# Qk-normed attention with a maxout FFN on one Trainium2 core: seven running rows per partition, and a new order of moves in the first batch

## The chip, the core and the metric

The kernel runs on one core of one Trainium2 chip. The core has five engines that work side by side, each with its own instruction list, which it takes in order: TensorE (PE in the profile, with PEld for its weight loads) multiplies matrices, VectorE (DVE) and ScalarE (ACT) work on whole tiles, GpSimd (POOL) does elementwise work beside them, and SyncE (SP) issues transfers. A transfer (DMA) runs on 16 DMA engines. SBUF is the core's memory with 128 partitions; PSUM is the small memory into which TensorE writes. The metric is device time in microseconds, from several executions, of which the median counts.

## The reference

Eight batches, twelve heads, 448 tokens, 64 features per head. Queries and keys are RMS-normed, softmax attention gives x (3584 tokens by 768), and three layers with a maximum between them and one output layer follow.

```
q_n, k_n = (rmsnorm(q, g_q), rmsnorm(k, g_k))
scores = scale * np.matmul(q_n, k_n.transpose(0, 1, 3, 2))
scores = scores - np.max(scores, axis=-1, keepdims=True)
attn = np.exp(scores)
attn = attn / (np.sum(attn, axis=-1, keepdims=True) + 1e-09)
return np.matmul(attn, v).astype(np.float32)
...
h = np.maximum(np.maximum(x @ w1, x @ w2), x @ w3)
return (h @ w_out).astype(np.float32)
```

All inputs and the output are fp32.

## The kernel before

**Pairs and beats.** The twelve heads of a batch make six pairs (NP = 6), so there are 48 pairs g over eight batches. The main loop runs beat(g, i) for twelve beats i of each pair. A beat issues a little of everything: work on pair g, the rest of pair w = g - 1, the preparation of pair n = g + 2, loads for pair g + 3, and a slice of the FFN of the batch before (thirds, which takes steps from a queue of generators). `clock` counts beats, `later(b, work)` puts work b beats further on, and `tick` issues what is due. The order in which the calls are made is the order of each engine's list (a schedule written out by hand), so what is issued first also runs first on its engine.

**Precision.** Batch 0 (g < PLAIN = 6) runs attention in fp32: rows are turned by TensorE (turn_whole L527/L532, copied by keep_whole L543/L550), scores are L663, the maximum over them L693 (row_max), the exponentials L709 on ScalarE, their turning L729 (turn_plain) with copies L742/L745 (keep_turned), attention times values L840 (add_values). From batch 1 on each operand is split into an fp16 upper and lower part: upper_rows and lower_rows split queries and keys, turn_rows (L512) turns both parts of 128 partitions by one transposing transfer, swap_keys (L519) writes the keys a second time with the two parts exchanged, scores are L671 and L678, upper_weights (L796) and lower_weights (L806) split the weights of attention into pp, which has three buffers, turn_weights (L819 and, for the last block by halves of 64 partitions, L825) turns them into pt, and add_values is L851.

**Rows.** Two heads of 448 rows make 896 rows, seven blocks of 128. In load_rows (L386, L389) a partition p takes row p of each block, so its seven rows are 128 rows apart, 256 bytes each. load_v (L425, L430) loads values in blocks of 128 tokens, five transfers for three pairs' worth. Block 3 holds the last 64 rows of one head and the first 64 of the other.

**Norms.** For pair n: squares (L443 on GpSimd from pair 2 on, L441 on ScalarE before), sum_squares (L450 on VectorE), inv_rms (L460 and a power L464 on GpSimd), scale_rows (L472, L481 on GpSimd).

**Weights.** The 24 blocks of the weight matrices (18 of the first layer, six of w_out) are loaded raw and prepared one by one in prep_block: rebias (L182, ScalarE), three steps of decode on VectorE (L190, L194, L199), then a bound over the block from TensorE products with itself (marks: L274 for the first layer in bound_in, L253 for w_out in bound_block), a maximum (L162), its spread over the partitions (most: L283, L337) and from it the scale (w_up: a power L293 on GpSimd; by and o_up for w_out in bound_out, L333 to L352). With the scale a block is split into two fp16 parts: upper on ScalarE (L303, L358), lower on VectorE (L306, L363). BLOCK_BEATS gives the beats at which blocks begin: one each 4 beats for the first 18, then one each 8 beats, the first of them after beat 72.

**Bounds of the values.** largest_v (L586 on TensorE into marks, then L162) and bound_v (L591, spread L597, clear L602 and L606, scale L610 and L614) give each batch's scale for v.

**FFN.** layer1 (L880) accumulates 18 matmuls of 448 columns into a PSUM tile acc, of which there are three buffers shared with marks, most, rows, turned and spread. hidden takes three accumulators: the first is copied to m (L890, ScalarE), the second gives max(acc, m) in m (L894), the third gives the maximum in acc itself, from which ScalarE writes the upper half of the hidden tile ht (L900) and VectorE the lower (L904). GpSimd copies the last 64 columns of ht to hx (L909). layer2 (L942) multiplies by w_out, result (L951) scales to osb, store (L918) writes out. The FFN of batch 0 enters the queue at pair 6, beat 6, that is beat 78.

Of the kernel before, what the change touches and what calls it, by code (L numbers as in the profile page):

```python
# [17 lines left out]
P = 128  # L18
# [16 lines left out]

BLOCK_BEATS = (4, 8)

# [11 lines left out]
def qknorm_attention_maxout_ffn_kernel(  # L49
# [107 lines left out]

    sums = [const.tile([P, 2 * UNITS], F32, name=f"ss{i}") for i in range(2)]


# [67 lines left out]
    def prep_block(n):  # L228
        kind, ft, j = blocks[n]
        raw = raws[n]  # L230
        f = plain(w_sb, n) if kind == "in" else plain(wo_sb, ft)
        rebias(raw)

        for stage in range(3):
            later(2 + stage, lambda stage=stage: decode(raw, f, stage), True)
        if kind == "out":
            bound_block(ft, f)
        later(5 if kind == "in" else 9, load_raw)
        if j == NJ - 1:
            later(5, lambda: bound_in(ft), True)  # L240
        elif kind == "out" and ft == NFT - 1:
            later(8, bound_out, True)

    def bound_block(ft, f):

        box = []

        def products():
            box.append(ps_m.tile([P, 512], F32, name="marks", tag="m"))
            halves = f.bitcast(BF16).rearrange("p (n t) -> p n t", t=2)  # L250
            for c in range(NCT):
                part = halves[:, c * P:(c + 1) * P, 1]
                nc.tensor.matmul(  # L253
                    box[0][:, 0:P], part, part, start=c == 0, stop=c == NCT - 1
                )

        later(6, products)
        later(8, lambda: row_largest(o_row[:, ft:ft + 1], box[0][:, 0:P]), True)

    def bound_in(ft):  # L260
# [55 lines left out]

        for at, work in ((2, products), (4, reduce), (5, spread), (7, clear)):
            later(at, work)


    def bound_out():
# [50 lines left out]

        for at, work in ((2, across), (3, spread), (5, scale)):
            later(at, work)
# [28 lines left out]
    def load_v(t):  # L403
# [8 lines left out]
        if b == 0:  # L412
# [10 lines left out]
            return  # L423
        for u in range(3):
            nc.sync.dma_start(  # L425
                out=vr[:, :, u],
                in_=rows[:, u * P:(u + 1) * P].rearrange("h p d -> p h d"),
            )
        for half, part in zip(HALVES, (rows[:, 3 * P:S], rows[:, 0:LEFT])):
            nc.sync.dma_start(out=vr[half, :, 3], in_=part.rearrange("h p d -> p h d"))  # L430

# [71 lines left out]
    def turn_rows(g, what):  # L503
        s = st[g]
        parts = s.pop(what + "p")
        if what == "k":
            t = sb.tile([P, 2, UNITS * P], F16, name="kt", bufs=2)
            to = t[:, 0].rearrange("p (n r) -> p n r", n=UNITS)
        else:
# [79 lines left out]
    def bound_v(b):  # L589
# [25 lines left out]

        later(2, spread)
        if b < SQUARED:
            later(3, clear)
        later(5 if b < SQUARED else 3, scale)

# [34 lines left out]
    def scores(g, c):  # L655
# [4 lines left out]
        if g < PLAIN:  # L660
# [5 lines left out]
            return  # L666
        keys = (slice(0, S), slice(S, 2 * S))
        if c < 3:
            for h in range(2):
                for n in range(2):  # L670
                    nc.tensor.matmul(  # L671
                        sc[:, h, :S], qt[:, 4 * h + c], kt[:, n, keys[h]],
                        start=n == 0, stop=n == 1,
                    )
        else:
            for n in range(2):
                for h, rows in enumerate(HALVES):
                    nc.tensor.matmul(  # L678
                        sc[rows, 0, :S], qt[:, 3, rows], kt[:, n, keys[h]],
                        start=n == 0, stop=n == 1,  # L680
                    )
# [205 lines left out]
    def hidden(b, acc, hs, ft, j, keep):  # L887
# [28 lines left out]
    def store(b, osb, row0, token, n, cols=slice(0, DO), on=nc.sync):  # L916
        first = b * S + token
        on.dma_start(out=out[first:first + n, cols], in_=osb[row0:row0 + n, cols])  # L918

# [165 lines left out]
    def beat(g, i):  # L1085
        w, n = g - 1, g + 2
        c, part = divmod(i, 3)
        k = 4 * g + c
        early = k + 1 <= 4 * PLAIN
        if part == 0:  # L1090
            if g < G:
                if k > 4 * PLAIN:
                    row_max(g, c)
                softmax(g, c)
            if early:
                scores(*divmod(k + 1, 4))
            if 0 < k <= 4 * PLAIN:
                turn_plain(*divmod(k - 1, 4))
            elif 0 < k <= 4 * G:
                lower_weights(*divmod(k - 1, 4))  # L1100
        if part == 1:
            if 0 < k <= 4 * PLAIN:
                keep_turned(*divmod(k - 1, 4))
            if PLAIN <= g < G:
                upper_weights(g, c)
        if part == 2:
            if early:
                row_max(*divmod(k + 1, 4))
            elif k + 1 < 4 * G:
                scores(*divmod(k + 1, 4))  # L1110
        if 0 <= w < PLAIN:
# [14 lines left out]
        if w >= 0 and i == (9 if w < PLAIN else 10):  # L1126
            finish(w, x_of[w // NP])
# [19 lines left out]
        if PLAIN <= n < G and i == 11:  # L1147
            upper_rows(n, "k")
        if n < G:
            if i in (0, 3):  # L1150
# [8 lines left out]
        if g == 0 and i in (0, 3):  # L1159
            load_v(i // 3)  # L1160
            later(8, lambda: largest_v(i // 3))
# [3 lines left out]
        if g == 1 and i == 1:  # L1165
            bound_v(0)
        if g > 1 and g % NP == 0 and g < G and i == 1:
            bound_v(g // NP)
        if PLAIN <= g < G and i == 9:
# [15 lines left out]
        if PLAIN <= g < G and i in (5, 8, 11):  # L1185
            turn_weights(g, i // 3 - 1)
        n_in = min(decoded[0], NFT * NJ)
        due_at = BLOCK_BEATS[0] * n_in + BLOCK_BEATS[1] * (decoded[0] - n_in)
        if decoded[0] < len(blocks) and clock[0] > due_at:
            later(0, lambda n=decoded[0]: prep_block(n), True)  # L1190
# [43 lines left out]
```

## Time and profile before

| | |
|---|---|
| time, median of 3 runs | 1021.29 us (1019.76 to 1024.45) |
| the profiled execution | 1023.19 us |
| its span, first to last instruction | 1021.3 us |
| TensorE busy, VectorE busy | 983.2 us, 693.2 us |
| mean granted TensorE clock | 0.984 |
| packets of DMA | 519548, of them under 512 bytes 494436 |

The profile is of one execution. A group of instructions is given by line, engine, operation and tiles (out<-in), count, busy time and mean duration; behind the second bar stands the idle time of the engine just before, with what ended it. "Waits" name who waited for whom. The granted clock is the share of full speed that TensorE was given; matmuls are pipelined, so their durations overlap.

### The profile page before, as it was taken

The page shows a single profiled execution, that of the slowest core. Times are in us where ns is not written, and L with a number is a line of the kernel's source. Part 1 is how long each engine was busy: PE and PEld are TensorE (multiplying, and loading weights), DVE is VectorE, ACT ScalarE, POOL GpSimd, SP SyncE. Part 2 cuts the span into 40 slices and gives each one's busy share as a digit, 9 for nine tenths or more (in the row PEclk, how much of TensorE's full clock was granted, in tenths as well). Part 3 has the DMA queues.
Part 4 walks back from the last instruction along what each step waited for, and adds up shares of the span by engine and source line. Part 5 has one row for each costly group of instructions (what it writes and reads, how often), then busy time and mean ns, then how long its engine had stood idle before and what let it go on. Part 6 is the DMA issues. An engine that isn't in the chain of part 4 may idle for free. (4 is left out here: it accounts for less than half of the span.)

```text
span 1021.3 us, 17511 instructions
## 1 busy us (share of the span) xinstructions
PE 983.2 (96%) x6045; PEld 528.8 (52%) x6045; DVE 693.2 (68%) x1341; ACT 624.1 (61%) x1419; POOL 600.9 (59%) x659
## 2 busy tenths in 40 slices
PE   8987789899999999999999999999999999999998
PEld 5554444445555555555555555555555555555554
DVE  6998998788667767776677666776767757660120
ACT  6787776477566676666656675667666666651111
POOL 7666786567666576666676765776666657310000
PEclk9998799899999999999999999999999999999999
DMA  9955899979989899999989999999989998851001
GB/s 241 232 165 156 192 177 206 162 136 173 203 170 176 164 210 191 171 175 179 195 162 180 171 195 185 184 165 184 197 154 181 177 195 137 144 94 56 1 1 62
DMA packets 519548, 165.94 MB, mean 162 GB/s; under 512 B 494436, under 2 KB 515236, under 8 KB 519460
## 3 DMA queue, kind: packets, MB, share of 16 engines
q1 hardware_dynamic: 456480, 148.83, 75.3%
q10 hardware_dynamic: 62980, 16.00, 8.4%
q8 instruction: 48, 0.79, 0.3%
q14 instruction: 40, 0.33, 0.1%
HBM read 53.28 MB, written 11.01 MB: 63 GB/s over the span
## 5 line engine op out<-in xcount | busy, mean ns | idle before, releaser
L880 PE MATMUL acc<-xt,w_sb 128*128 128x448 f16 x2592 | 516.0, 354 | 3.6 <-DVE ht L904 3.3
L880 PEld LDWEIGHTS <-w_sb 128*128 128x128 f16 x2592 | 251.4, 98 | 246.4 <-issue 18.0
L709 ACT ACTIVATE sc<-sc,nm 128x448 f32<-128x448 f32 x294 | 178.8, 608 | 190.0 <-DVE nm L693 185.4
L693 DVE TENSOR_REDUCE nm<-sc 128x2 f32<-128x896 f32 x192 | 186.2, 970 | 102.2 <-PE sc L671 59.5
L796 ACT ACTIVATE pp<-sc,rs 128x448 f16<-128x448 f32 x294 | 173.0, 633 | 79.1 <-ACT sc L709 36.3
L806 DVE SCALAR_TENSOR_TENSOR pp<-sc,rs,pp 128x448 f16<-128x448 f32 x294 | 188.0, 675 | 1.7 <-ACT pp L796 1.6
L464 POOL TENSOR_TENSOR ri<-ri,half_neg 128x7 f32<-128x7 f32 x96 | 146.5, 1526 | 8.0
L942 PE MATMUL acc<-w_sb,ht 128*128 128x384 f16 x864 | 147.9, 326 | 0.0
L498 POOL TENSOR_TENSOR kp<-kn,kp 128x448 f16<-128x448 f32 x42 | 43.6, 1037 | 161.4 <-ACT kp L492 154.8
L671 PE MATMUL sc<-kt,qt 128*128 128x448 f16 x504 | 116.7, 354 | 4.0 <-DVE pp L806 3.2
L942 PEld LDWEIGHTS <-ht 128*128 128x128 f16 x864 | 83.7, 98 | 59.2 <-issue 3.9
L671 PEld LDWEIGHTS <-qt 128*128 128x128 f16 x504 | 49.0, 98 | 50.2 <-issue 4.9
L851 PE MATMUL av<-pt,vp 128*64 128x448 f16 x672 | 73.0, 355 | 1.7 <-DMA pt<-pp 1.7
L909 POOL COPY hx<-ht 128x128 f16<-128x128 f16 x48 | 15.4, 321 | 95.0 <-DVE ht L904 93.9
L866 DVE SCALAR_TENSOR_TENSOR xt<-av,xt 128x448 f16<-128x448 f32 x42 | 26.2, 625 | 59.8 <-ACT xt L865 59.8
L638 POOL TENSOR_TENSOR vp<-vr,vp 128x512 f16<-128x512 f32 x42 | 50.0, 1192 | 21.0 <-ACT vp L632 21.0
L450 DVE TENSOR_REDUCE ss<-sq 128x7 f32<-128x448 f32 x96 | 57.7, 601 | 6.4 <-ACT sq L441 4.3
L498 POOL TENSOR_TENSOR qp<-qn,qp 128x448 f16<-128x448 f32 x42 | 45.6, 1086 | 22.8 <-ACT qp L492 21.8
L851 PEld LDWEIGHTS <-vp 128*64 128x64 f16 x672 | 36.0, 109 | 35.8 <-issue 16.7
L460 POOL TENSOR_SCALAR ri<-ss 128x7 f32<-128x7 f32 x54 | 17.8, 329 | 60.4 <-DVE ss L450 59.7
L894 DVE TENSOR_TENSOR m<-acc,m 128x448 f32<-128x448 f32 x48 | 29.5, 615 | 33.2 <-PE acc L880 33.0
L900 ACT ACTIVATE ht<-acc 128x448 f16<-128x448 f32 x48 | 26.2, 546 | 41.8 <-DVE acc L894 41.8
(136 smaller groups left out, 1189.3 us busy)
## 6 DMA issues: line engine op xcount, KB each, us to landing
raw<-in_moe_w_dram SPq DMA_DIRECT2D x18, 768.0 KB, 5.2
kt<-kt SPq DMA_DIRECT2D x84, 112.0 KB, 2.5
out_dram<-osb SPq DMA_DIRECT2D x24, 384.0 KB, 2.7
vr<-in_v_dram SPq DMA_DIRECT2D x42, 192.0 KB, 4.2
kr<-in_k_dram ACTq DMA_DIRECT2D x34, 224.0 KB, 3.6
qr<-in_q_dram ACTq DMA_DIRECT2D x34, 224.0 KB, 4.4
raw<-in_moe_w_out_dram SPq DMA_DIRECT2D x6, 768.0 KB, 5.1
vs<-vp SPq DMA_DIRECT2D x84, 48.0 KB, 2.3
```

The lines of the kernel that those rows point to most:

```text
L450: nc.vector.tensor_reduce(sums[g % 2][:, KQ[what]], sq, axis=AX, op=ALU.add)
L464: nc.gpsimd.tensor_tensor(out=ri, in0=ri, in1=half_neg[:, at], op=ALU.pow)
L498: nc.gpsimd.tensor_tensor(out=parts[:, :, 1], in0=n, in1=parts[:, :, 0], op=ALU.subtract)
L638: nc.gpsimd.tensor_tensor(out=vp[:, 1], in0=values_of(g).rearrange("p h n d -> p (h n) d"), in1=vp[:, 0], op=ALU.subtract,)
L671: nc.tensor.matmul(sc[:, h, :S], qt[:, 4 * h + c], kt[:, n, keys[h]], start=n == 0, stop=n == 1,)
L693: nc.vector.tensor_reduce(nm[:, :n], sc[:, :n, :S], axis=AX, op=ALU.max, negate=True)
L709: nc.scalar.activation(to, sc[:, h, :S], AF.Exp, bias=nm[:, h:h + 1], accum_out=total,)
L796: nc.scalar.activation(pp[:, h, 0], sc[:, h, :S], AF.Copy, scale=rs[:, h:h + 1])
L806: nc.vector.scalar_tensor_tensor(out=pp[:, h, 1], in0=sc[:, h, :S], scalar=rs[:, h:h + 1], in1=pp[:, h, 0], op0=ALU.mult, op1=ALU.subtract,)
L851: nc.tensor.matmul(av[half, :S], values, pt[:, 7 * h + block, SHIFT[h]:SHIFT[h] + S], start=n == 0, stop=n == len(steps) - 1,)
L880: nc.tensor.matmul(acc[:, :S], wt[:, wp, c], xs[c][:, xp], start=(c == 0 and n == 0), stop=(c == NCT - 1 and n == 2),)
L942: nc.tensor.matmul(acc[:, :HW], lhs, wo_sb[:, f, wp, half * HW:(half + 1) * HW], start=(f == 0 and n == 0), stop=(f == NFT - 1 and n == 2),)
```

## The change

**Layout from batch 1 on.** A partition takes seven rows that follow each other in memory. Queries, keys and values are then in another order of tokens: column r of block n is token 7r + n. turn_rows turns the queries by halves of 64 partitions, one head each; scores read a head's keys as seven pieces of 64 columns; load_v loads eight times 64 partitions; store writes each 64 rows of a batch after the first to every seventh row of the output.

```
-        rows = rows.rearrange("(n p) d -> p n d", p=P)
         if g < PLAIN:
+            rows = rows.rearrange("(n p) d -> p n d", p=P)
...
-            on[0].dma_start(out=t, in_=rows)
+            on[0].dma_start(out=t, in_=rows.rearrange("(p n) d -> p n d", p=P))
```

```
+        blocks = rows.rearrange("h (p n) d -> n p h d", n=UNITS)
+        for block in range(UNITS + 1):
             nc.sync.dma_start(
-                out=vr[:, :, u],
...
+                out=vr[HALVES[block % 2], :, block // 2], in_=blocks[block % UNITS]
+            )
```

```
             t = sb.tile([P, 8, P], F16, name="qt", bufs=2)
-            to = t[:, :UNITS]
-        nc.sync.dma_start_transpose(out=to, in_=parts.rearrange("p n a d -> p (n a d)"))
+            for h, half in enumerate(HALVES):
+                to = t.rearrange("p n r -> p (n r)")[:, h * S:(h + 1) * S]
+                nc.sync.dma_start_transpose(
+                    out=to.rearrange("p (n r) -> p n r", n=UNITS), in_=parts[half]
+                )
```

```
-                        sc[:, h, :S], qt[:, 4 * h + c], kt[:, n, keys[h]],
+                        sc[:, h, :S].rearrange("p (n r) -> p n r", n=UNITS),
+                        qt[:, h * (S + LEFT) + c * P:][:, :P], kt[:, n, :, half],
```

```
+        blocks = out[b * S:(b + 1) * S].rearrange("(p n) c -> n p c", n=UNITS)
+        for at in range(0, n, LEFT):
+            on.dma_start(
+                out=blocks[(token + at) // LEFT][:, cols],
+                in_=osb[row0 + at:row0 + at + LEFT, cols],
+            )
```

**Blocks.** The first 18 blocks begin as before; the six of w_out after beats 80, 86, 92, 99, 105 and 111, not 72, 80, 88, 96, 104 and 112.

```
-BLOCK_BEATS = (4, 8)
+BLOCK_BEATS = tuple(range(0, 72, 4)) + (80, 86, 92, 99, 105, 111)
...
-        for at, work in ((2, products), (4, reduce), (5, spread), (7, clear)):
+        for at, work in ((2, products), (4, reduce), (7, spread), (9, clear)):
...
-        for at, work in ((2, across), (3, spread), (5, scale)):
+        for at, work in ((2, across), (4, spread), (6, scale)):
```

In bound_block the products come after 7 beats (6 before) and the maximum after 9 (8); bound_out after 10 (8).

**Batch 0.** A new function is called at beats 2, 5, 8 and 11 of pairs 0 to 5, just ahead of row_max:

```
+    def follow():
+
+        here = sb.tile([1, 1], F32, name="here", bufs=4)
+        nc.vector.memset(here, 0.0)
+        nc.gpsimd.tensor_copy(seen, here)
```

The copy on GpSimd waits for the memset on VectorE. In these pairs squares are at beats 2 and 5 (0 and 3 before), sum_squares at 4 and 7 (2 and 5), inv_rms at 5 and 8 (5 and 7), scale_rows of k at 8 (8) and of q at 11 (9), or 9 for a pair from batch 1 on. The turning of the last scores of a pair (turn_plain, c = 3) is at beat 11 of that pair, its copy (keep_turned) at beat 0 of the next; before, they stood at beats 0 and 1 of the next. add_values is at beat 2 (4 before), finish of pair 0 at beat 10 (9).

```
+        if i == 0 and 0 < g <= PLAIN:
+            keep_turned(w, 3)
...
+                if g < PLAIN:
+                    follow()
                 row_max(*divmod(k + 1, 4))
...
+            if i == 11:
+                turn_plain(g, 3)
...
-        if w >= 0 and i == (4 if w < PLAIN else 7):
+        if w >= 0 and i == (2 if w < PLAIN else 7):
             add_values(w)
```

**Bounds of v.** largest_v comes 10 and 11 beats after the first two loads (8 before). bound_v of batch 0 is at beat 4 of pair 1 (1 before), that of a later batch at beat 7 of the last pair of the batch before (beat 1 of its own first pair before). Its spread is 4 beats later, not 2, for later batches, and clear and scale follow at 6 and 9 (3 and 5), or the scale at 5 where there is no clear.

**The maximum of batch 0.** The third accumulator's maximum goes into m, not into the accumulator:

```
-        most = m if j == 1 else acc[:, :S]
+        most = m if j == 1 or b == 0 else acc[:, :S]
```

More of the change, by code (lines that the diff above doesn't have):

```diff
@@ L158, in qknorm_attention_maxout_ffn_kernel @@
     sums = [const.tile([P, 2 * UNITS], F32, name=f"ss{i}") for i in range(2)]
+    seen = const.tile([1, 1], F32, name="seen")
+    def follow():
+        here = sb.tile([1, 1], F32, name="here", bufs=4)
+        nc.vector.memset(here, 0.0)
+        nc.gpsimd.tensor_copy(seen, here)
     def row_largest(dst, src):
@@ L241, in prep_block @@
         elif kind == "out" and ft == NFT - 1:
-            later(8, bound_out, True)
+            later(10, bound_out, True)
     def bound_block(ft, f):
@@ L255, in products @@
                 )
-        later(6, products)
-        later(8, lambda: row_largest(o_row[:, ft:ft + 1], box[0][:, 0:P]), True)
+        later(7, products)
+        later(9, lambda: row_largest(o_row[:, ft:ft + 1], box[0][:, 0:P]))
     def bound_in(ft):
@@ L614, in scale @@
             nc.vector.reciprocal(v_up[:, b:b + 1], v_down[:, b:b + 1])
[L616 to L619, printed above, removed]
+        if b >= SQUARED:
+            later(4, spread)
+            later(5, scale)
+            return
+        for at, work in zip((4, 6, 9) if b else (2, 3, 5), (spread, clear, scale)):
+            later(at, work)
     def scale_v(g):
@@ L666, in scores @@
             return
-        keys = (slice(0, S), slice(S, 2 * S))
+        qt = qt.rearrange("p n r -> p (n r)")
+        kt = kt.rearrange("p a (n r) -> p a n r", n=UNITS)
         if c < 3:
-            for h in range(2):
+            for h, half in enumerate(HALVES):
                 for n in range(2):
                     nc.tensor.matmul(
-                        sc[:, h, :S], qt[:, 4 * h + c], kt[:, n, keys[h]],
+                        sc[:, h, :S].rearrange("p (n r) -> p n r", n=UNITS),
+                        qt[:, h * (S + LEFT) + c * P:][:, :P], kt[:, n, :, half],
                         start=n == 0, stop=n == 1,
@@ L676, in scores @@
             for n in range(2):
-                for h, rows in enumerate(HALVES):
+                for h, half in enumerate(HALVES):
                     nc.tensor.matmul(
-                        sc[rows, 0, :S], qt[:, 3, rows], kt[:, n, keys[h]],
+                        sc[half, 0, :S].rearrange("p (n r) -> p n r", n=UNITS),
+                        qt[:, 3 * P:S + LEFT][:, half], kt[:, n, :, half],
                         start=n == 0, stop=n == 1,
@@ L916, in store @@
     def store(b, osb, row0, token, n, cols=slice(0, DO), on=nc.sync):
-        first = b * S + token
-        on.dma_start(out=out[first:first + n, cols], in_=osb[row0:row0 + n, cols])
+        if b == 0:
+            on.dma_start(out=out[token:token + n, cols], in_=osb[row0:row0 + n, cols])
+            return
+        blocks = out[b * S:(b + 1) * S].rearrange("(p n) c -> n p c", n=UNITS)
[4 more added lines that the diff above has]
+            )
     o_scale = const.tile([P, B], F32, name="o_scale")
@@ L1096, in beat @@
                 scores(*divmod(k + 1, 4))
[L1097 to L1098 removed]
+            if g < PLAIN:
+                if c > 0:
+                    turn_plain(g, c - 1)
+            elif k == 4 * PLAIN:
+                pass
             elif 0 < k <= 4 * G:
@@ L1101, in beat @@
         if part == 1:
-            if 0 < k <= 4 * PLAIN:
-                keep_turned(*divmod(k - 1, 4))
+            if c > 0 and g < PLAIN:
+                keep_turned(g, c - 1)
             if PLAIN <= g < G:
@@ L1125, in beat @@
         thirds(of[i] + (len(queue) > 1 and i % 6 == 4))
-        if w >= 0 and i == (9 if w < PLAIN else 10):
+        if w >= 0 and i == (9 if 0 < w < PLAIN else 10):
             finish(w, x_of[w // NP])
@@ L1148, in beat @@
             upper_rows(n, "k")
-        if n < G:
+        if g < PLAIN:
+            if i in (2, 5):
+                squares(n, "kq"[i // 3])
+            if i == 11:
+                turn_plain(g, 3)
+            if i in (4, 7):
+                sum_squares(n, "kq"[i // 7])
+            if i in (5, 8):
+                if i == 8:
+                    scale_rows(n, "k")
+                inv_rms(n, "kq"[i // 8])
+            if i == (9 if n >= PLAIN else 11):
+                scale_rows(n, "q")
+        elif n < G:
             if i in (0, 3):
@@ L1160, in beat @@
             load_v(i // 3)
-            later(8, lambda: largest_v(i // 3))
+            later(10 if i == 0 else 11, lambda: largest_v(i // 3))
         if g % 3 == 0 and g + 6 < G and i == 9:
@@ L1164, in beat @@
             later(8, lambda: largest_v(g // 3 + 2))
-        if g == 1 and i == 1:
+        if g == 1 and i == 4:
             bound_v(0)
-        if g > 1 and g % NP == 0 and g < G and i == 1:
-            bound_v(g // NP)
+        if g % NP == NP - 1 and g + 1 < G and i == 7:
+            bound_v(g // NP + 1)
         if PLAIN <= g < G and i == 9:
@@ L1186, in beat @@
             turn_weights(g, i // 3 - 1)
-        n_in = min(decoded[0], NFT * NJ)
-        due_at = BLOCK_BEATS[0] * n_in + BLOCK_BEATS[1] * (decoded[0] - n_in)
-        if decoded[0] < len(blocks) and clock[0] > due_at:
+        if decoded[0] < len(blocks) and clock[0] > BLOCK_BEATS[decoded[0]]:
             later(0, lambda n=decoded[0]: prep_block(n), True)
```

7 lines of the change are left out of this document (3 added, 4 removed).

## The prediction

> **What bounds the kernel now.** I read the page's busy line and its forty slices first, to see which engine limits which part of the span.
>
> ```profile
> PE 983.2 (96%) x6045; PEld 528.8 (52%) x6045; DVE 693.2 (68%) x1341; ACT 624.1 (61%) x1419; POOL 600.9 (59%) x659
> ```
>
> ```profile
> PE   8987789899999999999999999999999999999998
> ```
>
> ```profile
> PEclk9998799899999999999999999999999999999999
> ```
>
> TensorE is busy 96% of the span, and all its digits below 9 lie in the first eight slices (a slice is 25.5 us) and the last. The same holds for its clock. So I asked for busy time by stage (columns: length, then PE, PEld, DVE, ACT, POOL busy with counts, clock, DMA share, GB/s).
>
> ```profile
> 25.00:118.00 93.00, 81.10 (x580) 46.30 (x580) 86.01 (x120) 73.05 (x163) 63.60 (x56) 0.91 0.70 182
> 118.00:150.00 32.00, 24.79 (x144) 13.96 (x145) 30.71 (x58) 22.46 (x51) 24.46 (x23) 0.89 0.97 197
> 150.00:180.00 30.00, 28.54 (x186) 15.11 (x184) 26.15 (x50) 20.67 (x46) 20.08 (x21) 1.00 0.97 204
> 180.00:240.00 60.00, 53.16 (x318) 26.76 (x315) 49.36 (x93) 38.33 (x83) 38.94 (x41) 0.94 0.87 151
> ```
>
> ```profile
> 260.00:400.00 140.00, 138.60 (x838) 74.42 (x837) 95.77 (x197) 90.41 (x210) 92.01 (x104) 1.00 0.99 187
> 400.00:600.00 200.00, 199.74 (x1222) 105.82 (x1221) 141.95 (x291) 130.00 (x302) 133.37 (x153) 1.00 0.97 178
> ```
>
> From 260 us on TensorE has nothing to gain: 0.26 us idle in 200. Before that there are two stages. From 25 to 118 us (pairs 1 to 5 of batch 0) VectorE is busy 86.0 of 93 us and sets the pace. From 118 to 240 us VectorE is still full at first (30.7 of 32), and TensorE loses 15.5 us idle. As TensorE runs its list in a fixed order to the end, a microsecond saved before 240 us comes off the end. The waits of TensorE in 118 to 260 us name the places (total, times, longest), and those after 260 us show what is left there:
>
> ```profile
> PE most L597 <- DVE v_most L591: 4.9, 1, 4.9
> PE acc L880 <- DVE ht L904: 3.3, 1, 3.3
> ...
> PE most L283 <- DVE most L162: 1.4, 1, 1.4
> PE marks L586 <- DVE o_up L342: 1.3, 1, 1.3
> ```
>
> ```profile
> PE av L851 <- DMA pt<-pp: 1.7, 3, 1.2
> ```
>
> **The change, part by part. Pairs 1 to 5.** The groups of VectorE in 25 to 118 us, and the same lines over the whole run (minimum/median/maximum ns):
>
> ```profile
> L199 DVE SCALAR_TENSOR_TENSOR w_sb<-raw,w_sb 128x768 uint32<-128x768 uint32 x16 | 18.0, 1126 | 0.1
> L194 DVE SCALAR_TENSOR_TENSOR w_sb<-raw,w_sb 128x768 uint32<-128x768 uint32 x15 | 17.2, 1148 | 0.3
> L693 DVE TENSOR_REDUCE nm<-sc 128x2 f32<-128x896 f32 x15 | 16.2, 1081 | 0.0
> L306 DVE SCALAR_TENSOR_TENSOR w_sb<-w_sb,w_up 128x768 f16<-128x768 f32 x12 | 12.8, 1062 | 0.0
> L190 DVE TENSOR_SCALAR w_sb<-raw 128x768 uint32<-128x768 uint32 x15 | 11.4, 758 | 0.0
> ```
>
> ```profile
> L190 DVE TENSOR_SCALAR w_sb<-raw x24: 542/562/1412, 17.9 to 197.6; 128x768 uint32<-128x768 uint32 x24
> L194 DVE SCALAR_TENSOR_TENSOR w_sb<-raw,w_sb x24: 941/959/1596, 18.5 to 198.2; 128x768 uint32<-128x768 uint32 x24
> L199 DVE SCALAR_TENSOR_TENSOR w_sb<-raw,w_sb x24: 937/958/1772, 20.9 to 202.9; 128x768 uint32<-128x768 uint32 x24
> L306 DVE SCALAR_TENSOR_TENSOR w_sb<-w_sb,w_up x18: 1000/1009/1664, 47.7 to 160.5; 128x768 f16<-128x768 f32 x18
> ```
>
> One form, one size, but a third of them take 0.6 us more. Against the minimum the stage loses 16 x (1126-937) + 15 x (1148-941) + 12 x (1062-1000) + 15 x (758-542) ns = 10.1 us. The partner is GpSimd: its squares are stretched in the same stage, against 400 to 800 us (second row).
>
> ```profile
> L443 POOL TENSOR_TENSOR sq<-qr 128x448 f32<-128x448 f32 x5 | 6.8, 1353 | 0.0
> ```
>
> ```profile
> L443 POOL TENSOR_TENSOR sq<-qr 128x448 f32<-128x448 f32 x22 | 20.5, 934 | 0.0
> ```
>
> follow() makes GpSimd wait at beats 2, 5, 8 and 11 until VectorE is at its maximum over scores, and the squares (2, 5) and multiplications (8, 11) are moved there. That maximum reads scores, not the weight blocks, and shows no stretching (1081 ns is its mean). It lasts about as long as a GpSimd operation at three of the four beats; at beat 8 it covers one bank only. GpSimd starts somewhat after it, so a tail sticks out. I take half: **-5.0 us** (ends 0 and -10.1).
>
> The trace has no rule for who yields. The Trainium skill, "SBUF — State Buffer", section "SBUF: two separate sides", says that VectorE and GpSimd share a port pair, held for a whole instruction by whichever starts first, and that only two-port or two-SBUF-input VectorE operations need it; the stretched rows above fit. By it three of four covers are free, and the term would be an estimated -7.6.
>
> The price of follow() is 24 VectorE memsets, 20 of them in this stage. The nearest row is a memset at the start:
>
> ```profile
> 0.92 0.06 DVE L140 MEMSET ones_c<- 128x1 f32 x1
> ```
>
> That is 20 x 0.06 = **+1.2 us** on the full engine. The 24 copies on GpSimd lie in its spare 29.4 us. Behind a waiting copy stand GpSimd's powers and multiplications, and TensorE's transposes of rows wait for those; they come 5 beats ahead of it.
>
> VectorE also stands idle here, since TensorE is late:
>
> ```profile
> DVE most L162 <- PE marks L274: 3.3, 2, 2.6
> DVE v_rows L162 <- PE marks L586: 3.0, 2, 1.6
> ```
>
> Turning the last scores inside the pair, av at beat 2 not 4, and the v marks two or three beats later act on these 6.3 us. I take **-2.0** (0 to -6.3). ScalarE is busy 73.1 of 93 us, so it is next, with room. Stage: -5.8.
>
> **118 to 240 us.** bound_v(1) moves from beat 73 to beat 67 and its matmul comes four beats later, so the 4.9 us wait goes. VectorE is full there, though, and the next scores wait for it all the same. What helps VectorE is that the first second-layer block moves from beat 73 to 81: 0.54+0.94+0.94 = 2.4 us less in pair 6. I take **-2.4** for both (0 to -4.9). The spread of the weight bound, two beats later, saves **-1.0** of the 1.4 (0 to -1.4).
>
> The 3.3 us wait is an accumulator held until both halves of the hidden layer are read out. For batch 0 the maximum now goes into m, so the accumulator is free after the maximum. After this wait the clock was halved, as after the gap before 62.3 us:
>
> ```profile
> 62.30 1.02 PE L663 MATMUL sc<-kt,qt 64*128 64x448 f32 x4 [2.94 <-ACT e L709]
> ```
>
> ```profile
> 190.88 2.40 PE L880 MATMUL acc<-xt,w_sb 128*128 128x448 f16 x6 [3.29 <-DVE ht L904]
> ```
>
> ```profile
> 63.50:66.90 3.40, 3.40 (x14) 1.85 (x14) 3.40 (x6) 3.33 (x10) 1.17 (x2) 0.50 0.62 177
> ```
>
> ```profile
> 189.80:196.60 6.80, 5.72 (x16) 2.31 (x16) 3.41 (x8) 3.42 (x7) 5.43 (x8) 0.50 0.73 142
> ```
>
> Half clock for 6.8 us costs 3.4 more. Of 6.7 I take **-5.0** (0 to -6.7), as VectorE may hold it otherwise. The Trainium skill, "TensorE: Matmul & The Clock Gate", section "What's actually happening", asks for an idle window of about 3.4 us before the clock halves. Gaps of 2.94 and 3.29 sufficed here, so the measurement decides; by the page the clock's 3.4 would not hang on this gap, and the term would be an estimated -1.6.
>
> Of the 1.3 us at the output bound, spread and scaled a beat later, I take **-0.5** (0 to -1.3). Stage: -8.9.
>
> **From batch 1 on.** Contiguous rows replace small pieces in 84 loads; no wait of TensorE above names a load of q or k: 0. New on SyncE per pair: one more turning of q by halves, one more v transfer (eight for five, each third pair), and half a store. The nearest rows:
>
> ```profile
> L825 SPq DMA_TRANSPOSE pt<-pp x84: 1193/1256/2419, 148.9 to 919.2; - x84
> ```
>
> ```profile
> L430 SPq DMA_DIRECT2D vr<-in_v_dram x28: 620/664/1453, 25.9 to 766.7; - x28
> ```
>
> L825 has two issues in each of 42 pairs, so a pair lasts (919.2-148.9)/41 = 18.8 us, and 1.26 + 0.66 + 0.33 = 2.2 us of it are new. SyncE's longest wait shows that it often waits for data itself:
>
> ```profile
> SPq L819 <- DVE pp L806: 99.5, 54, 4.9
> ```
>
> So 0; the upper end is a rival below. Behind them in SyncE's list stand pt's turnings; q itself is turned at beat 3 and used at beat 11.
>
> The keys are now read as seven pieces of 64. No row shows this. Nearest are matmuls that read every second element, against whole ones:
>
> ```profile
> 34.27 1.21 PE L274 MATMUL marks<-w_sb 128*128 128x128 bf16 x18
> ```
>
> ```profile
> 145.77 1.30 PE L880 MATMUL acc<-xt,w_sb 128*128 128x448 f16 x6
> ```
>
> 1.21/18 = 67 ns for 128 columns and 1.30/6 = 217 ns for 448, each with one drain in it: a column costs about as much strided. So 0; below nothing there is no reason for a gain.
>
> **The sum:** -5.8 - 8.9 = -14.7. The profiled execution took 1023.19 us (span 1021.3, 1.9 around it), 0.2% above the median of 1021.29. From the profile that gives 1008.5, from the median 1006.6; I forecast **1007 us**, 1000 to 1014 by the terms' likelier halves.
>
> **The rivals.**
> *The stretching only moves* (0.12): GpSimd's tail meets the next block step. For: beat 8's cover lasts half as long. Against: GpSimd has 29 us to spare. Stage one gives +1.2, so 1021.3 + 1.2 - 8.9 = 1014.
> *Every gap closes and the clock stays up* (0.11): TensorE's half clock in stage one is gone with the gaps, and VectorE gains the whole 10.1 + 6.3 - 1.2 = 15.2. For: 0.91 clock there; against: three engines over 78% busy. 1021.3 - 15.2 - 8.9 = 997.
> *It does not do what it says* (0.15): GpSimd, tied to VectorE, hands over w_up later, ScalarE waits in its order, and 2.4 us return in each of five pairs: 1007 + 12 = 1019.
> *SyncE becomes the bound, slower* (0.09): the 2.2 us stand ahead of pt's turnings, in 42 pairs; pt late holds its source pp, of which there are three, and so ScalarE's next weights. For: TensorE already waits for pt, 1.7 us. Against: that is all in 42 pairs. Above 14.7/42 = 0.35 us per pair let through the change loses; at one, 1007 + 42 = 1049.
> *Reading pieces costs columns, slower* (0.03): six breaks in 504 matmuls and in 84 side-by-side couples are 3528, so 4.2 ns a break eat the gain; at 10 ns, 1042.
>
> **How the numbers follow.** The forecast keeps 0.50. About 0.5% (5.1 us, below 1016.2 or above 1026.4) is what a measurement here can tell. Faster: 0.50 + 0.11 + 0.10 of the first rival = 0.71. Same: 0.15 + 0.02 = 0.17. Slower: 0.12. The range 996 to 1022 leaves out the slower cases and the edges of the others; all terms at their best would be 992.
>
> **What would show it.** Right: L190, L194 and L199 near their minima before 118 us; no 4.9 and no 3.3 us wait of TensorE; clock 1.00 at 190 us; after 260 us TensorE's idle and its pace unchanged. Wrong: TensorE waiting for pt or kt in later batches (SyncE), slower L671, or ScalarE waiting for w_up.

## The result, and the profile after

The changed kernel takes 1064.11 us (median of 5 runs, 1062.12 to 1065.64) against 1021.29: ratio 1.0405, 95% interval 1.038 to 1.0429. It is slower by 42.8 us, where 14 us less were forecast. The profiled span is 1063.6 us.

The busy line of the page after, and its row of the clock in forty slices:

```profile
PE 992.5 (93%) x6045; PEld 534.2 (50%) x6045; DVE 699.3 (66%) x1365; ACT 623.7 (59%) x1419; POOL 604.8 (57%) x683
...
PEclk9999899999899999999899998999999999999999
```

TensorE is idle for 1063.6 - 992.5 = 71.1 us, where it was 1021.3 - 983.2 = 38.1, and its own work, the same 6045 matmuls, lasts 9.3 us longer. Both together are the 42.3 us that the span grew.

Busy time by stage of the kernel after (columns as before):

```profile
25.00:118.00 93.00, 80.18 (x599) 47.75 (x600) 89.35 (x151) 78.03 (x175) 67.45 (x81) 0.97 0.70 196
118.00:150.00 32.00, 23.85 (x143) 12.23 (x140) 29.64 (x53) 20.17 (x44) 26.47 (x27) 0.88 0.83 169
...
180.00:240.00 60.00, 54.24 (x337) 28.39 (x335) 53.12 (x98) 39.52 (x86) 44.01 (x43) 0.97 0.79 155
...
260.00:400.00 140.00, 130.88 (x768) 69.27 (x767) 89.33 (x181) 84.01 (x195) 86.40 (x97) 0.96 0.87 168
400.00:600.00 200.00, 192.93 (x1139) 100.86 (x1136) 134.07 (x274) 119.69 (x279) 124.24 (x141) 0.98 0.89 167
```

The loss lies where TensorE had nothing to lose: from 260 us on it now stands idle 9.1 us of 140 and 7.1 of 200, and its clock is below 1. TensorE's waits after, from 260 to 900 us, say for what:

```profile
PE av L870 <- DMA pt<-pp: 24.9, 12, 4.4
PE sc L688 <- DVE pp L825: 4.7, 5, 1.4
```

The turned weights pt come late; before, these were three waits of 1.7 us in all. Most pairs are not touched. Let a pair last from its first maximum on VectorE to that of the next pair. Then the ten pairs that follow a load of values (13, 16, ... 40) are 45.6 us longer together than before, and the other 25 of pairs 12 to 46 are 1.5 us shorter. So the whole loss lies behind the loads. Pair 19 is one of the ten. VectorE's timeline shows its first maximum and that of pair 20, before and then after:

```profile
375.84 1.09 DVE L693 TENSOR_REDUCE nm<-sc 128x2 f32<-128x896 f32 x1 [0.87 <-PE sc L671]
...
395.39 1.08 DVE L693 TENSOR_REDUCE nm<-sc 128x2 f32<-128x896 f32 x1
```

```profile
381.99 1.09 DVE L712 TENSOR_REDUCE nm<-sc 128x2 f32<-128x896 f32 x1 [0.88 <-PE sc L688]
...
402.60 0.63 DVE L712 TENSOR_REDUCE nm<-sc 128x1 f32<-128x448 f32 x1 [6.38 <-PE sc L696]
408.62 1.08 DVE L712 TENSOR_REDUCE nm<-sc 128x2 f32<-128x896 f32 x1
```

The pair lasted 19.6 us and lasts 26.6. Just ahead of it the values of three later pairs are loaded. SyncE's timeline there, before (start, duration, what it issues, how many):

```profile
371.99 2.57 SPq L425 DMA_DIRECT2D vr<-in_v_dram  x3
374.60 1.37 SPq L430 DMA_DIRECT2D vr<-in_v_dram  x2
376.08 2.43 SPq L819 DMA_TRANSPOSE pt<-pp  x1
378.61 0.57 SPq L918 DMA_DIRECT2D out_dram<-osb  x1
...
387.88 1.20 SPq L519 DMA_DIRECT2D kt<-kt  x2
389.17 6.22 SPq L819 DMA_TRANSPOSE pt<-pp  x3
395.81 0.76 SPq L649 DMA_DIRECT2D vs<-vp  x1
```

Already here, in the rows left out too, no gap of more than about 0.1 us lies between two rows until 395.39 us. And after:

```profile
380.08 6.32 SPq L437 DMA_DIRECT2D vr<-in_v_dram  x8
386.51 3.15 SPq L838 DMA_TRANSPOSE pt<-pp  x1
389.75 1.18 SPq L941 DMA_DIRECT2D out_dram<-osb  x2
391.03 0.65 SPq L665 DMA_DIRECT2D vs<-vp  x1
391.73 0.64 SPq L666 DMA_DIRECT2D vs<-vp  x1
392.48 1.25 SPq L519 DMA_TRANSPOSE kt<-kp  x1
393.82 2.53 SPq L844 DMA_TRANSPOSE pt<-pp  x2
396.44 2.52 SPq L524 DMA_TRANSPOSE qt<-qp  x2
399.08 0.52 SPq L937 DMA_DIRECT2D out_dram<-osb  x1
399.64 0.60 SPq L941 DMA_DIRECT2D out_dram<-osb  x1
400.35 1.38 SPq L533 DMA_DIRECT2D kt<-kt  x2
401.82 6.33 SPq L838 DMA_TRANSPOSE pt<-pp  x3
```

The reader is to see that each row begins a tenth of a microsecond after the one above it ends. For 28 us SyncE waits for no other engine, and whatever is added to this list makes all that stands below it late. The rows themselves differ, too: the first turning of pt takes 3.15 us to issue, where one of kt takes 1.25. TensorE's timeline after, at the place where the turnings of 393.82 should have been there:

```profile
390.68 2.43 PE L899 MATMUL acc<-xt,w_sb 128*128 128x448 f16 x12
396.54 0.58 PE L870 MATMUL av<-pt,vp 128*64 128x448 f16 x1 [3.42 <-DMA pt<-pp]
397.77 3.15 PE L870 MATMUL av<-pt,vp 128*64 128x448 f16 x15 [0.65 <-DMA pt<-pp]
```

It waits 3.42 us, and then fifteen matmuls last 3.15 us; in pair 13 of the kernel before, at 275.20 us, they took 1.67. The busy time by stretch after has the reason (the granted clock is the number behind POOL's count):

```profile
395.00:400.00 5.00, 2.81 (x14) 1.48 (x16) 1.17 (x3) 1.16 (x2) 0.70 (x2) 0.54 0.56 92
```

So one late turning is paid twice. From 260 to 900 us the granted clock is 0.98 on average, where it was 1.00. The Trainium skill, "TensorE: Matmul & The Clock Gate", section "What's actually happening", gives one idle window of about 3.4 us for this. This gap is as long, but the clock is at half from 395.4 us on, 2.3 us after the gap began, and gaps of 2.94 and 3.29 us in the kernel before were already enough.

### The profile page after: what moved, and what is told of

The parts are those of the page before. It is cut to its first block, busy times and chain, and to the rows that moved or that the text cites. A ratio compares the mean times of both kernels' runs of the same rounds, so it can differ in the third digit from the quotient of the medians.

```text
span 1063.6 us, 17840 instructions
## 1 busy us (share of the span) xinstructions
PE 992.5 (93%) x6045; PEld 534.2 (50%) x6045; DVE 699.3 (66%) x1365; ACT 623.7 (59%) x1419; POOL 604.8 (57%) x683
## 2 busy tenths in 40 slices
DMA packets 457391, 165.97 MB, mean 156 GB/s; under 512 B 421524, under 2 KB 453076, under 8 KB 457300
## 5 line engine op out<-in xcount | busy, mean ns | idle before, releaser
L815 ACT ACTIVATE pp<-sc,rs 128x448 f16<-128x448 f32 x294 | 173.0, 633 | 129.5 <-DMA pt<-pp 68.5
L825 DVE SCALAR_TENSOR_TENSOR pp<-sc,rs,pp 128x448 f16<-128x448 f32 x294 | 187.9, 675 | 5.4 <-ACT pp L815 5.3
L870 PE MATMUL av<-pt,vp 128*64 128x448 f16 x672 | 82.9, 381 | 25.1 <-DMA pt<-pp 24.9
L870 PEld LDWEIGHTS <-vp 128*64 128x64 f16 x672 | 40.2, 116 | 63.2 <-issue 33.8
L913 DVE TENSOR_TENSOR m<-acc,m 128x448 f32<-128x448 f32 x54 | 33.1, 613 | 33.1 <-PE acc L899 33.0
L490 POOL TENSOR_TENSOR qn<-qn,gain 128x448 f32<-128x448 f32 x42 | 48.9, 1164 | 3.3
L808 DVE TENSOR_SCALAR rs<-sc 128x2 f32<-128x2 f32 (+1 forms) x168 | 25.9, 154 | 34.2 <-ACT sc L728 34.1
```

Source lines behind the costliest of these rows:

```text
L815: nc.scalar.activation(pp[:, h, 0], sc[:, h, :S], AF.Copy, scale=rs[:, h:h + 1])
L825: nc.vector.scalar_tensor_tensor(out=pp[:, h, 1], in0=sc[:, h, :S], scalar=rs[:, h:h + 1], in1=pp[:, h, 0], op0=ALU.mult, op1=ALU.subtract,)
L870: nc.tensor.matmul(av[half, :S], values, pt[:, 7 * h + block, SHIFT[h]:SHIFT[h] + S], start=n == 0, stop=n == len(steps) - 1,)
```

## The experiments

**Order and layout apart.** The diff falls in two: what runs when (with blocks, batch 0 and bounds), and the layout from batch 1 on (load_rows, load_v, turn_rows, scores, store). e1 has the first alone, e2 the second alone.

> The new order of batch 0 and of the blocks, with the old layout of rows, values, queries and stores. Theory S (SyncE's list is too long from batch 1 on, so pt is turned late): the 7.2 us that pair 6 begins earlier (118.61 to 111.40 us) stay to the end, about 1013 us (1008 to 1018), and TensorE's waits for pt fall from 24.9 to about 2 us. Rival O (the loss comes from the new order: the blocks of w_out from beat 80 on and batch 0's moves push VectorE's work into the later pairs): 1040 us or more, with pair 9 beginning later than 205.9 us.

> The new layout alone, with the old order of batch 0 and of the blocks. Theory S: the whole loss without the gain, 1021 + 43 + 7 = 1071 us (1060 to 1080), TensorE waiting for pt 20 us or more. Rival O: about 1021 us (1016 to 1026).

e1: 1021.2 us, ratio 1.0002 (0.9991 to 1.0012). e2: 1061.9 us, ratio 1.04 (1.0374 to 1.0426). The layout is the whole loss, as theory S said of e2, and the order's forecast gain is nowhere: e1 lies outside both ranges. Waits of TensorE and of ScalarE in e2:

```profile
PE av L861 <- DMA pt<-pp: 26.2, 17, 4.1
```

```profile
ACT pp L806 <- DMA pt<-pp: 69.8, 29, 4.7
```

They are those of the kernel after (24.9 and 68.5), without any of the new order.

**Where the order's gain went.** The quotes call K the theory that w_out's new beats collide with GpSimd's work. In e1 pair 6 begins at 110.99 us (118.61 before), but the rest comes back before 260 us. The weight blocks' groups of VectorE from 118 to 260 us, before and in e1:

```profile
L199 DVE SCALAR_TENSOR_TENSOR w_sb<-raw,w_sb 128x768 uint32<-128x768 uint32 x7 | 7.9, 1122 | 0.0
L306 DVE SCALAR_TENSOR_TENSOR w_sb<-w_sb,w_up 128x768 f16<-128x768 f32 x7 | 7.8, 1107 | 0.0
L194 DVE SCALAR_TENSOR_TENSOR w_sb<-raw,w_sb 128x768 uint32<-128x768 uint32 x7 | 7.7, 1095 | 0.1
L363 DVE SCALAR_TENSOR_TENSOR w_sb<-w_sb,o_block 128x768 f16<-128x768 f32 x6 | 7.3, 1222 | 0.2 <-ACT w_sb L358 0.2
```

```profile
L201 DVE SCALAR_TENSOR_TENSOR w_sb<-raw,w_sb 128x768 uint32<-128x768 uint32 x6 | 10.3, 1721 | 0.0
L206 DVE SCALAR_TENSOR_TENSOR w_sb<-raw,w_sb 128x768 uint32<-128x768 uint32 x6 | 9.0, 1499 | 0.1
L370 DVE SCALAR_TENSOR_TENSOR w_sb<-w_sb,o_block 128x768 f16<-128x768 f32 x6 | 8.5, 1420 | 0.4 <-ACT w_sb L365 0.2
L313 DVE SCALAR_TENSOR_TENSOR w_sb<-w_sb,w_up 128x768 f16<-128x768 f32 x6 | 8.2, 1361 | 0.2 <-ACT w_sb L310 0.2
```

Six steps of each now take 10.3 + 9.0 + 8.5 + 8.2 = 36.0 us; at the means of before it would be 27.3. The same instructions at new beats are stretched, and TensorE waits for VectorE. That GpSimd's operations stretch them is argued from the first stage, not shown. e6 is e1 with the old places of w_out's blocks:

```
-BLOCK_BEATS = tuple(range(0, 72, 4)) + (80, 86, 92, 99, 105, 111)
+BLOCK_BEATS = tuple(range(0, 72, 4)) + (72, 80, 88, 96, 104, 112)
...
-        for at, work in ((2, across), (4, spread), (6, scale)):
+        for at, work in ((2, across), (3, spread), (5, scale)):
```

and in bound_block and bound_out the old 6, 8 and 8 beats.

> The new order of batch 0 with the old layout, and the six blocks of w_out at their old beats (72, 80, 88, 96, 104, 112) with the old distances inside them. Theory K (the new beats put the blocks' steps beside GpSimd's large operations: L201 took 1721 ns and L206 1499 in 118 to 260 us, against 1095 and 1122 before, 8.7 us in all with the two scaling lines, and so gave back what pairs 1 to 5 gained): the steps fall back to some 1100 ns and about 1013 to 1017 us remain. Rival F (VectorE is full up to 240 us, so what it gains early it waits out later, wherever the blocks stand): 1018 to 1024 us, as with the new beats.

1017.61 us (10 runs), ratio 0.9966 (0.9949 to 0.9982), between the ranges of K and F: the four steps take 29.5 us, and some of the gain stays. e12 takes follow() out of e6 as well.

> The new order of batch 0 with old layout and w_out's old beats (1017.6 us with it), without follow(): GpSimd is not held to VectorE. If follow() earns what the forecast gave it (-5.0 + 1.2 = -3.8 us) the time goes back to 1020-1022 us and L194's line stretches again above 1100 ns; if the gain came from the moved TensorE work and the places of the squares alone, it stays within 1.5 us of 1017.6.

1019.38 us, ratio 0.9972 (0.9957 to 0.9986), in neither range: at the end there is no difference that the intervals can tell. Pair 6 begins at 113.67 us in e12 and at 110.76 in e6, but the traces of all runs with e6's first stage spread from 110.8 to 114.1, so what follow() earns is not shown.

**The layout's three splits, each on the kernel before.** Queries turned by halves, values in eight transfers, each store of 128 rows as two of 64; the addresses in memory stay the old ones.

```
-        nc.sync.dma_start_transpose(out=to, in_=parts.rearrange("p n a d -> p (n a d)"))
+            for half in HALVES:
+                nc.sync.dma_start_transpose(out=to[:, :, half], in_=parts[half])
```

```
         for u in range(3):
+            for h, half in enumerate(HALVES):
+                first = u * P + h * LEFT
                 nc.sync.dma_start(
-                    out=vr[:, :, u],
-                    in_=rows[:, u * P:(u + 1) * P].rearrange("h p d -> p h d"),
+                    out=vr[half, :, u],
+                    in_=rows[:, first:first + LEFT].rearrange("h p d -> p h d"),
```

```
+        for at in range(0, n, LEFT):
+            on.dma_start(
+                out=out[first + at:first + at + LEFT, cols],
+                in_=osb[row0 + at:row0 + at + LEFT, cols],
+            )
```

> The kernel before, only that the queries are turned by two transfers of 64 partitions instead of one of 128, as the new layout needs it; all else as before. Theory S: 1.25 us more of SyncE in each of 42 pairs, of the 2.2 us added: 15 to 35 us slower, 1036 to 1056 us, with pt late. If it is the values' eight transfers or the stores that matter, within 5 us of 1021.

> The kernel before, only that later batches' values come in eight transfers of 64 partitions at the same beat, not five. Theory B: three more issues of 0.66 us in each third pair, just where the list is longest: 6 to 20 us slower (1027 to 1041), in jumps at those pairs. Rival E: 14 x 2.0 us spread over 42 pairs with room, within 4 us of 1021.

> The kernel before, only that each store of 128 rows is issued as two of 64. Theory B: 24 more issues of some 0.6 us at places that fall beside the values' transfers only now and then: 0 to 8 us slower. Rival E: 24 x 0.6 = 14 us of issue, of which less than 5 us show.

e4: ratio 1.0116 (1.0087 to 1.0145). e7: 1.0136 (1.0104 to 1.0168). e8: 1.0121 (1.0091 to 1.0152). Together 3.73%, against the 4.0% of the layout: if the three add, they are the price, and what is left for the addresses and the keys' pieces is within the intervals. Two of the three sizes were missed: e4 (1031.3 us) lies below theory S's range, e8 (1033.6) above both, and only e7 (1035.1) is in theory B's. e4 adds half a turning to every one of 42 pairs, and still the ten pairs behind a load are 14.0 us longer, the other 25 of pairs 12 to 46 are 4.9 us shorter. Where the list has room, the added issue costs nothing.

**Is it SyncE's time to issue, or the transfers?** Five runs on the kernel after move issues or take them off SyncE: e3 issues values and stores from ScalarE's queue, e9 the stores alone, e10 turns the queries at beat 6 (not 3), e5 spreads the eight transfers over beats 6, 7, 9 and 10 of two pairs, and e11 is e5 with e9, e10 and the old places of w_out's blocks. B2 in the quotes is SyncE's time to issue, C that the price stays though SyncE is relieved.

```
-            on.dma_start(
+            nc.scalar.dma_start(
...
-                if i in (2, 3):
-                    turn_rows(g + 1, "kq"[i - 2])
+                if i in (2, 6):
+                    turn_rows(g + 1, "kq"[i // 6])
...
-        if g % 3 == 0 and g + 6 < G and i == 9:
-            load_v(g // 3 + 2)
+        if g % 3 < 2 and g - g % 3 + 6 < G and i in (6, 7, 9, 10):
+            load_v_part(g // 3 + 2, 4 * (g % 3) + (6, 7, 9, 10).index(i))
```

> The changed kernel with the transfers of values and the stores of later batches issued by ScalarE instead of SyncE; the transfers themselves are the same. Theory S: SyncE loses 8/3 x 0.66 + about 0.6 us = 2.4 us a pair, a little more than the 2.2 us that the change added, so the loss goes: 1013 to 1025 us, ScalarE's waits for pt back to some 13 us from 68.5. Rival D (it is the transfers, smaller and of 64 partitions, that crowd the DMA engines, not their issue): still 1055 us or more.

> The changed kernel with the stores of batches 1 to 7 issued by ScalarE, which makes their data; values stay on SyncE. Theory B2 (SyncE's list is full from end to end in the pairs that hold the values' transfers, most of all where stores fall in too; each issue more there delays pt, and TensorE by about as much): 42 issues leave SyncE, so at least the 12.4 us of the split stores come back and some of the others: 1064 to 1035-1052 us. Rival D (the transfers themselves crowd the DMA engines): 1060 or more.

> The changed kernel with the queries turned at beat 6, behind the first turning of weights of the pair, not at beat 3 ahead of it. As many issues. Theory B2 (a full list, the place matters little when the list has no gap): 1064 falls by less than 8 us. Rival P (it is the place of the second turning, ahead of pt's, that costs): the 11.9 us of the halves come back, 1048 to 1054 us.

> The changed kernel; only the eight transfers of values are no longer issued in one beat of each third pair, but one each at beats 6, 7, 9 and 10 of two pairs. As many issues as before. Theory B (SyncE's list overflows only in each third pair, where the eight transfers stand together ahead of pt's turning; the run with the layout alone loses in jumps after pairs 12 and 15, 5.7 and 3.5 us): the ten such pairs after pair 11 lose nothing more, 1064 falls to 1016 to 1032 us, and ScalarE's waits for pt from 68.5 to below 30 us. Rival E (every pair pays for its longer list, wherever the issues stand): 1050 us or more.

> The changed kernel with all of it: values spread over two pairs, stores of batches 1 to 7 on ScalarE, queries turned at beat 6, and w_out's blocks at their old beats. Theory B2: the list fits in every pair again, so the layout costs 0 to 10 us, and with the order's -3.6 us that gives 1015 to 1030 us; the layout itself brings nothing below 1017. Rival C (reading the keys in pieces, or the smaller transfers, cost by themselves): 1040 or more.

e3: 1098.39 us, ratio 1.0758 (1.0731 to 1.0784). e9: 1062.61 us, 1.0389 (1.0359 to 1.042). e10: 1061.0 us, 1.0375 (1.0338 to 1.0412). e5: 1051.95 us, 1.0295 (1.0262 to 1.0328). e11: 1050.41 us, 1.0276 (1.0241 to 1.0311). Four of the five missed the ranges that the time to issue had named and fell into those of the rivals; only e10 came out as B2 said. Spreading the values takes back some 12 us and no more, since the loss moves with them: the ten pairs behind a load are 26 us shorter than in the kernel after, the others 15 us longer. The stores, 49 issues and not 42, gave nothing, which spoke against the time to issue. e3 shows a price on the other side; waits of ScalarE there:

```profile
ACT osb L977 <- DMA vr<-in_v_dram: 35.3, 4, 9.6
```

ScalarE issues in the order of its work, so an issue that has to wait holds its weights. With that price these runs could not separate the two theories.

**The two apart.** In the quotes of this last set A is the time to issue and D the transfers. f1 adds three issues of 16 bytes to each group of values of the kernel before, f5 ten of 4 bytes: time to issue with next to no data. f2 has e7's transfers, with SyncE issuing five of eight as before. f3 and f4 take the two copies a pair that shift the values (vs<-vp) off SyncE, in the kernel after and in e6. f6 joins f3 with e5 and the old places.

```
+        small = const.tile([1, 10], F32, name=f"small{t}")
+        for i in range(10):
+            nc.sync.dma_start(out=small[:, i:i + 1], in_=rows[0, i:i + 1, 0:1])
...
-                nc.sync.dma_start(
+                (nc.sync, nc.scalar)[h].dma_start(
...
-        nc.sync.dma_start(out=t[lower], in_=vp[upper, :, 0:3])
-        nc.sync.dma_start(out=t[upper], in_=vp[lower, :, 1:4])
+        nc.gpsimd.dma_start(out=t[lower], in_=vp[upper, :, 0:3])
+        nc.gpsimd.dma_start(out=t[upper], in_=vp[lower, :, 1:4])
```

> The kernel before; behind the five transfers of a group of values (twelve groups) SyncE issues three more of 16 bytes each, which nothing reads. The same number of added issues, in the same place, as in the run with the values in eight, and no bytes to speak of. Theory A (SyncE's time to issue is what costs: its list is without a gap in these pairs): as with eight, 1035 us (1030 to 1038), ratio 1.008 to 1.016. Theory D (the transfers over 64 partitions crowd the DMA engines and so delay the turnings): 1019 to 1024, ratio 0.998 to 1.003.

1020.82 us, ratio 0.9983 (0.9969 to 0.9998): no loss, a miss for A. SyncE's timeline in f1, at the same group as above:

```profile
375.09 1.05 SPq L433 DMA_DIRECT2D small<-in_v_dram  x3
376.25 1.33 SPq L822 DMA_TRANSPOSE pt<-pp  x1
```

The three took 1.05 us, and the turning behind them 1.33 where it had taken 2.43: as if part of that turning's issue were a wait, which the small issues used up. So f1 had been too small a dose.

> The kernel before with ten issues of 4 bytes behind the five transfers of a group of values: at 0.25 us each 2.5 us of SyncE in twelve pairs, as much as the split in eight added there (5.2 us for eight, 2.8 to 3.2 for five), and no bytes to speak of; the three small issues before were only 1.05 us, and the turning behind them took 1.33 us of SyncE where it had taken 2.43. Theory A (SyncE's time to issue): as the split in eight, 1030 to 1038 us. Theory D (the transfers; a turning's issue waits for them anyway, and the added issues go into that wait): up to the 1.2 us a group that the wait does not cover, 1020 to 1029 us, and at the middle 1023.

1046.63 us, ratio 1.0243 (1.0218 to 1.0267). SyncE's timeline in f5, and then TensorE's waits for pt:

```profile
384.09 3.62 SPq L433 DMA_DIRECT2D small<-in_v_dram  x10
387.81 1.68 SPq L822 DMA_TRANSPOSE pt<-pp  x1
```

```profile
PE av L854 <- DMA pt<-pp: 16.9, 19, 3.9
```

Forty bytes a group cost 23.9 us, above what either theory named, since ten issues lasted 3.62 us and not 2.5. That is 2.0 us for each of the twelve groups. In e7 the group's issues last 6.0 us where they took 4.0, and it costs 13.9 / 12 = 1.16 us.

> The kernel before with the values in eight transfers, three of which ACT issues: SyncE issues five, as before, and the transfers are those of the run with eight (1035 us). Theory A: 1019 to 1025 us, plus what ACT pays for 36 issues of about 0.4 us, most of it beside its waits. Theory D: 1032 to 1038 us. Both right in part: between, 1026 to 1031.

1027.94 us, ratio 1.0059 (1.0037 to 1.008): with the transfers of e7 but five issues on SyncE as before, a bit more than half of e7's price is gone. ScalarE's queue now issues, and `ACT osb L953 <- DMA pt<-pp` waits 7.7 us there.

The traces of these runs show what the price goes by. Here is SyncE's time for a group of values, with the small issues, and for the turning of weights behind it (means over the eleven groups whose next issue is one, us); the last column is the loss of the run divided by twelve groups.

| | the group | the turning | both | more than before | loss a group |
|---|---|---|---|---|---|
| before | 3.9 | 2.6 | 6.7 | | |
| f1 | 4.7 | 1.6 | 6.4 | -0.26 | -0.14 |
| f2 | 4.1 | 2.9 | 7.3 | 0.65 | 0.45 |
| e7 | 5.9 | 2.3 | 8.3 | 1.65 | 1.16 |
| f5 | 7.8 | 1.8 | 9.7 | 3.06 | 1.99 |

Small issues shorten the turning behind them by about a microsecond. What is added to both together is paid at some 0.7 us for each microsecond, in f2 and e7, where the transfers are smaller, as in f5, where there is hardly any data. What makes one turning longer to issue than another is not shown; there the transfers may have their part.

> The kernel after, with the two copies a pair that shift the values (vs<-vp, 0.62 us of SyncE each) issued by GpSimd: SyncE has 1.24 us less to issue in every pair, about what the second half of the queries' turning added. Theory A: about that half's price comes back, 1047 to 1055 us. Theory D: 1061 to 1067 us. GpSimd's own price for 84 issues can add up to some 5 us to both.

1044.23 us, ratio 1.022 (1.0186 to 1.0253), against 1.0405: 84 issues of 0.62 us less give back 1.85%, some 19 us, more than theory A had asked for.

> The new order with the old layout and the old places of w_out's blocks (1017.6 us so far), with the same two copies issued by GpSimd. Theory A: the pairs that hold values (19.6 to 20.4 us against 18.6) shorten to 18.6: 1008 to 1013 us. Theory D: 1016 to 1022 us.

1015.75 us, ratio 0.9933 (0.9908 to 0.9959), the fastest of all, but short of theory A's range; pair 19 lasts 18.6 us, where it lasted 20.4 in e6. The intervals of the two touch, so the step from e6 to f4 is likely, not shown; that both beat the kernel before is.

> The kernel after with the values' eight transfers spread over four beats of two pairs, the old places of w_out's blocks, and the two shifting copies a pair issued by GpSimd. If the reliefs add (spread -12.2 us, copies -19.9, places -3.6, each against the kernel after): 1028 us, 1023 to 1033, still above the kernel before and 10 us above the order alone. If they take away the same lateness: 1038 to 1046 us.

1037.51 us, ratio 1.0135 (1.0103 to 1.0168): between the two cases named. The reliefs share part of the lateness that they remove, and 17 to 20 us of the layout's price stay above e6.

So A is shown: added time of SyncE, with hardly any data, makes the turnings late (f5), and issues taken off SyncE give it back (f3). D is not excluded beside it. That almost nothing came from e9 stays open; in its trace the ten pairs behind a load are 4.2 us shorter than in the kernel after, and the others 2.7 us longer. Turning the queries whole in the new layout and a fourth buffer of pp were not tried.

## Why the prediction was wrong

**The step that failed: SyncE's 2.2 us a pair at 0.** The issues were counted and sized rightly: half a turning of queries takes as long as the whole one (1244 ns after, 1248 for the whole of L512 before; the 1256 of L825 was itself a half), a transfer of values 624 ns (0.66 taken). The cover was wrong. It was read from SyncE's largest wait, 99.5 us in 54 times over the whole run. From pair 12 to 44 these waits are 64.8 us: 46.3 lie in the third pair of each group (14, 17, ... 44), just ahead of the next load, 10.2 in the pairs behind a load, and none in pairs 13, 19 and 31. There the list had no gap already before, which SyncE's timeline of pair 19 would have shown. Behind a load the three splits add some 2.3 us of values, 1.3 of queries and the second halves of stores, and each of the ten pairs there loses 4.6 us on average.

The rival "SyncE becomes the bound" named the chain: turnings late, pp held, ScalarE's next weights late. That its 42 us meet the measured 42.8 is luck: the microsecond a pair was an example, spread over 42 pairs, while ten pairs carry the loss. It was held unlikely because TensorE waited for pt only 1.7 us in 42 pairs, again a sum over the run.

**Stage one, -5.8: -7.2.** Pair 6 begins at 111.40 us, not 118.61. By terms, from e1 and at the counts of before: the weight blocks' stretching fell by 2.4 us (-5.0 taken); the price of follow() was exact:

```profile
L164 DVE MEMSET here<- 1x1 f32 x20 | 1.2, 59 | 0.0
```

VectorE's idle fell from 7.0 to 3.2 us (-2.0 taken), and of the rest 1.1 us is one block step that now lies behind the pair. These terms leave about 1 us unexplained. Only one of the three steps of decode came near its minimum, as the signs had asked (L194's, 968 ns in e1; the others took 1166 and 701). Without follow() (e12) pair 6 begins 4.9 us earlier than before, so most of the gain came from the work moved ahead, and GpSimd being led has at most the rest.

**118 to 240 us, -8.9: a loss.** What was said of the waits came true. TensorE's waits from 118 to 260 us after:

```profile
PE sc L688 <- DVE pp L825: 12.1, 7, 2.8
PE marks L600 <- DVE o_row L169: 3.0, 1, 3.0
```

The 4.9 and the 3.3 us are gone, though the clock still falls to half near 190 us, for 3.4 us where it was 6.8. But `sc <- DVE pp` rose from 3.0 to 12.1: VectorE set the pace there, as the prediction noted for the v bound, and the step that failed here is that the later blocks of w_out were counted as relief without asking what their steps cost at the new beats. They cost 8.7 us of VectorE (e1), of which the old places take 6.5 back (e6). Even then pair 6 begins 7.9 us early and pair 12 only 6.7, so the stage gains nothing, and the term of the waits, too, was VectorE's time and not TensorE's.

**Right at 0:** the keys in seven pieces. Groups of the page after, scores and attention:

```profile
L688 PE MATMUL sc<-kt,qt 128*128 128x448 f16 x504 | 116.3, 353 | 18.4 <-DVE pp L825 16.8
...
L870 PE MATMUL av<-pt,vp 128*64 128x448 f16 x672 | 82.9, 381 | 25.1 <-DMA pt<-pp 24.9
```

A score matmul takes 353 ns (354 before). The contiguous loads gained nothing that these runs show: 457391 packets for 519548, and no wait of TensorE that a load of q or k ended.

## What to carry to other kernels

A queue's cover is to be read in the stretch with most on its list, not from its waits summed over the run: follow one such pair's timeline and look whether each row begins where the last one ended. A layout that needs more, smaller DMAs pays on the queue that issues them, and what is late is what stands behind them. A block of work moved to relieve one engine can take longer at its new place, and its price is read there.

## What the runs showed of the hardware

An issue of 4 bytes took SyncE a median of 0.25 us and one of 96 KB 0.62; the turning of half the partitions took as long as the whole one. The issue of a turning of weights (L838 after) lasted from 1.3 to 4.3 us; behind a group of values it took 2.6 us on average before, behind small issues 1.6 (f1).

The Trainium skill, "DMA: Bandwidth & Descriptors", section "Rules for kernel authors", advises against two transfers to disjoint halves of the partitions, since they run one after the other, and says that spreading DMAs over engines only saves time to issue. The advice agrees with e4, e7 and e8 (1.2 to 1.4% each); f5 shows that time to issue alone has such a price, with no halves at all. For the second, issuing from GpSimd saved (f3), while from ScalarE it cost another 3.5% (e3), as the issues waited in that engine's order.
